# Moving one input load ahead in a DMA queue, and regrouping the reads of an output bank, in a Mamba2 + maxout kernel

## The chip, the cores and the metric

The kernel runs on one core of a Trainium2 chip. The metric is device time of one execution in microseconds (us); the median of three runs of the kernel before is 284.18 us (284.13 to 284.55). Engines are called as in the profile: PE (TensorE matmul), PEld (its weight loads), DVE (VectorE), ACT (ScalarE), POOL (GpSimd), SP (SyncE, which here only issues DMAs). An "SPq" row is the issue of a DMA by SP's sequencer, not its transfer.

## The reference

Two stages follow each other. The first is a chunked state-space scan over 4 sequences, 8 heads, 768 tokens, head width 32 and state width 16. The second is a feed-forward layer with a maximum over three products, on 3072 tokens of width 256:

```
cum = cumsum(log(clip(a)));  L = exp(cum_i - cum_j), causal
y   = ((C B^T) * L) x  +  (C state) * exp(cum)
state = exp(cum_last) * state + sum_j B_j x_j exp(cum_last - cum_j)
x = y as (3072, 256)
h = max(max(x w1, x w2), x w3)          # d_ff = 768
out = h w_out
```

## The kernel before

**Tiling.** The tokens of every sequence are cut into six chunks of 128 (c = 0 to 5). While the feed-forward of chunk c runs on PE, the scan of chunk c + 1 is threaded between its products. The order of all work is written out by hand: the instructions of each engine stand in the order in which the program calls the functions, and every engine goes through its own list in order. Waits between engines are put in by the framework from the tiles that an instruction reads and writes; a PSUM tile counts as a whole, so a write to one quarter of a bank waits for a read of another quarter.

**Chunk 0's feed-forward** is the loop over n (lines 977 to 1038). Among its products it issues the loads of chunk 2 through SP at n = 3 (lines 1011 to 1017) and n = 11 (line 1026): `B`, two weight pieces (`fetch`), the first half of the decay rows `L` (`decay_load`, 1 MB), the eight small loads of `E` (`last_load`), the second half of `L`, `x`, and `C`. `C` has a single buffer (`raw_C`, line 125), so its load of chunk 2 waits until PE has transposed chunk 1's `C` (`scan_tc`, line 428, at n = 11).

**Chunks 1 to 5** follow plans of words (lines 1054 to 1077): FIRST for chunk 1, STEADY for 2 to 4, LAST for 5. One row of a plan is one step k = 0 to 5. The first row of FIRST and the rows k = 3 to 5 of STEADY are

```
"E w tc g L load c e m01"                  # FIRST, k = 0
"E 1 w x2 D L D 1 m23"                     # FIRST, k = 1
"E 2 z1 D D L A D D"                       # STEADY, k = 3
"E 1 y 4 z1 D D L n23 z1"                  # STEADY, k = 4
"E z2 D L 1"                               # STEADY, k = 5
```

- `E` is `early` (line 668): eight products into the banks sumA (one buffer) and sumB (two), then the ACT copy of line 678 and the DVE additions of lines 679 to 681.
- `L` is `late` (line 684): six more products into the same banks, then on even k the ACT copy of line 690, on odd k the DVE maximum of line 707 (`raised`), which read sumA; and the DVE addition of line 695. Another maximum over the other three quarters (line 707 again, 128x768) is put off to the next pop.
- a digit pops that many put-off DVE instructions; `w` is `weight_sums` (DVE line 634, then POOL lines 640 to 643).
- `tc` transposes `C` of the next chunk (line 424), `g` transposes a piece of a weight (723, ACT copy 727), `c` scales that transpose into `CT` (ACT, 439), `e` takes exp of `E` (ACT, 443), `load` issues the loads two chunks ahead.
- `m` and `n` words are the causal masks on POOL (`decay_masks`, line 398); `x` and `z` words are the exponentials of the decays (`decay_part`, ACT, line 405, four instructions a part), which follow the masks of the same tile.
- `y` are the scan's output products (lines 520 and 533).
- `D` is `down_next`: for chunks 1 to 4 it calls `down_seven` (line 793), one seventh of the output product for a pair of sequences u. The sevenths come in the order p = 1, 7, 5, 6, 2, 4, 3, in one PSUM bank `o` of four quarters (line 791 has the quarter of each; p = 2 adds to the quarter of p = 1, p = 4 and 3 to those of 7 and 5). Two pairs make fourteen `D` words per chunk. In STEADY the seventh `D` (p = 3) stands in k = 2, the eighth and ninth (p = 1 and 7) side by side in k = 3, the twelfth and thirteenth (p = 2 and 4) side by side in k = 4, and the fourteenth (p = 3) in k = 5.

In `down_seven` the bank `o` is read at four of the sevenths: after p = 1 by the ACT copy of line 807, after p = 6 by three DVE additions (line 812) of which each takes the result of the one before, after p = 2 by the ACT copy of line 814, and after p = 3 by the DVE addition of line 816, which is followed by the DMA to the output.

Of the kernel before, what the change touches and what calls it, by code (L numbers as in the profile page):

```python
# [19 lines left out]
def kernel(  # L20
# [70 lines left out]
    def ffn_bank(shape, name):  # L91
        turn["ffn"] += 1
        if shared["ffn"] and turn["ffn"] % 3:
            return bank("sumB", 2, shape, name)
        return bank("ffn", 1, shape, name)
# [26 lines left out]
    def load(c, name):  # L122
        src, w = sources[name]
        t = blocks[c][name] = raw.tile(
            [P, BH, w], FP32, tag="raw_" + name, bufs=1 if name == "C" else 2,
            name="raw_" + name)
        nc.sync.dma_start(
            out=t, in_=src[:, :, c * P:(c + 1) * P, :].rearrange("b h s n -> s (b h) n"))
# [70 lines left out]
    def decode():  # L199

        first, second = decode_steps()
        first()
        unsigned.append(second)

    def sign():

        unsigned.pop(0)()
# [69 lines left out]
    def from_last(rows, cum, name):  # L277

        fj = passing(cum)
        for w in range(cum.shape[1]):  # L280
            nc.scalar.activation(
                fj[0:rows, w], cum[0:rows, w], AF.Exp, bias=cum[0:rows, w, P - 1:P], scale=-1.0)
        return fj
# [23 lines left out]
    def decays(c):  # L307
        Ls[c] = att.tile([P, NB, NH, P], FP32, tag="L", name="L")
        return Ls[c]
# [73 lines left out]
    def decay_load(c, pairs=(0, 2)):  # L383
        L = decays(c) if 0 in pairs else Ls[c]
        for b in pairs:
            nc.sync.dma_start(
                out=L[:, b:b + 2].rearrange("j b h i -> j (b h) i"),
                in_=cums[b * NH:(b + 2) * NH, c, :].partition_broadcast(P))

    def last_load(c):  # L390
        E = blocks[c]["E"] = raw.tile([HN, NB, P], FP32, tag="E", name="E")
        rows = cums[:, c].rearrange("(b h) s -> h b s", h=NH)
        for h in range(NH):
            nc.sync.dma_start(out=E[h * N:(h + 1) * N], in_=rows[h].partition_broadcast(N))
# [143 lines left out]
    def first_own(bs):  # L538

        y = att_bank([P, KD, 2, P], "y")  # L540
        for b in bs:
            for h in range(NH):
                t, q = divmod(h, QH)
                nc.tensor.matmul(
                    out=y[q * D:(q + 1) * D, t, b % 2], lhsT=blocks[0]["x"][:, b * NH + h],
                    rhs=L0[:, b, h], start=(b % 2 == 0 and t == 0), stop=True,
                    tile_position=(0, q * D), skip_group_check=True)
        if 0 not in yT:
            yT[0] = ffn.tile([P, KD, BLK], FP32, tag="yT", bufs=3, name="yT")
        r = bs[0] // 2  # L550
        nc.scalar.copy(
            out=yT[0][:, :, r * HB:(r + 1) * HB], in_=y.rearrange("p t b i -> p t (b i)"))
# [29 lines left out]
    def h_of(c):  # L582
        if c not in hT:
            hT[c] = ffn.tile([P, NF, BLK], FP32, tag="h", name="h")
        return hT[c]

    def group(bank, i, f, halves):

        for r in halves:
            for k in range(KD):  # L590
                nc.tensor.matmul(  # L591
                    out=bank[:, r * HB:(r + 1) * HB],
                    lhsT=w_sb[i][:, k, f * P:(f + 1) * P],
                    rhs=yT[0][:, k, r * HB:(r + 1) * HB],
                    start=(k == 0), stop=(k == KD - 1), skip_group_check=True)

    def whole_group(bank, i, f):
        for k in range(KD):
            nc.tensor.matmul(  # L599
                out=bank, lhsT=w_sb[i][:, k, f * P:(f + 1) * P], rhs=yT[0][:, k],  # L600
                start=(k == 0), stop=(k == KD - 1))
# [59 lines left out]
    def pop(n):  # L661
        while n and later:
            later.pop(0)()
            n -= 1
# [97 lines left out]
    def right(p, pair):  # L762

        def part(k, d):
            w = based["G"] if pair == 0 else wo_sb[:, 2 * pair - 2:2 * pair]
            return w[:, k, d * P:(d + 1) * P]

        if p in (1, 2, 4):
            return part(*{1: (0, 0), 2: (1, 0), 4: (1, 1)}[p])
        return seven[p][:, pair]  # L770
# [22 lines left out]
    def down_seven(c, u, p):  # L793

        if p == 1:
            held["o"] = ffn_bank([P, 4, P], "o")
            held["du"] = ffn.tile([P, 3, P], FP32, tag="du", bufs=1, name="du")
            held["out"] = ffn.tile([P, 2, DM], FP32, tag="ob", bufs=2, name="ob")
        o, du, ob = held["o"], held["du"], held["out"]
        flat = ob.rearrange("p b m -> p (b m)")  # L800
        for pair in range(NQ + 1):
            x = sides[c][p] if pair == 0 else zs[c, pair - 1][p]
            nc.tensor.matmul(  # L803
                out=o[:, SLOT[p]], lhsT=x[:, u * P:(u + 1) * P], rhs=right(p, pair),
                start=(p == 1 and pair == 0), stop=True, skip_group_check=True)
        if p == 1:
            nc.scalar.copy(out=du[:, 0], in_=o[:, 0])
        if p == 6:
            for to, one, two in (
                    (du[:, 1], o[:, 1], du[:, 0]), (du[:, 2], o[:, 2], du[:, 1]),  # L810
                    (flat[:, 3 * P:4 * P], o[:, 3], du[:, 2])):
                nc.vector.tensor_tensor(out=to, in0=one, in1=two, op=ALU.add)
        if p == 2:
            nc.scalar.copy(out=flat[:, 0:P], in_=o[:, 0])
        if p == 3:
            nc.vector.tensor_tensor(
                out=flat[:, P:3 * P].rearrange("p (s m) -> p s m", s=2), in0=o[:, 2:4],
                in1=du[:, 1:2].to_broadcast([P, 2, P]), op=ALU.add)
            nc.sync.dma_start(
                out=out.rearrange("(b s) m -> s b m", s=S)[c * P:(c + 1) * P, u::2],  # L820
                in_=ob)
# [126 lines left out]
    def part(c, n=1):  # L948
        for _ in range(n):
            if parts.get(c):  # L950
                decay_part(*parts[c].pop(0))

    def first_tokens():
        from_js = by_token(R, fj, "from_js", 1.0, att_bank)
        for c in range(1, NC):
            ncum[c], from_j[c] = ncums[:, :, c], from_js[:, :, c]
# [20 lines left out]
    for n in range(NF * 3):  # L977
        j, g = divmod(n, 2)
        q, i = divmod(j, 3)
        f = 2 * q + g  # L980
        if n == 0:
            pair = [ffn_bank([P, BLK], "up") for _ in range(2)]
            group(pair[0], 0, 0, (0,))
            first_own((2, 3))
            group(pair[1], 0, 1, (0,))
            for p, ff in zip(pair, range(2)):
                group(p, 0, ff, (1,))
        if j > 0:
            p = ffn_bank([P, BLK], "up")
            whole_group(p, i, f)  # L990
        else:
            p = pair[g]
        if i == 0 and g == 0:
            m = ffn.tile([P, 4, HB], FP32, tag="m", name="m")
        if n in (13, 14, 16, 17):
            pop(2)
        mg = m[:, 2 * g:2 * g + 2].rearrange("p r t -> p (r t)")
        if i == 0:
            nc.scalar.copy(out=mg, in_=p)
        else:  # L1000
            nc.vector.tensor_tensor(
                out=mg if i == 1 else h_of(0)[:, f], in0=mg, in1=p, op=ALU.max)
        if g == 0 and n <= 16:
            sign()
            if n <= 14:
                decode()
        if n == 1:
            fj = from_last(R, a_sb, "fj")
        if n == 3:
            first_tokens()  # L1010
            load(2, "B")
            fetch()
            fetch()
            decay_load(2, (0,))
            last_load(2)
            decay_load(2, (2,))
            load(2, "x")
            decay_masks(1, (0, 1))
        if n == 9:
            decay_masks(1, (2, 3))  # L1020
        if n in (5, 7, 9, 11, 13, 14, 15, 16):
            part(1)
        if n == 11:
            transposed(1)
            scan_c(1)
            load(2, "C")
        if n == 12:
            scan_e(1)
            scan_cd(1)
            scores(1, 0)  # L1030
        if n == 15:
            shared["att"] = False
            scores(1, 2)
            places()
            weight_sums(0)
        if n == 17:
            decode()
            weight_sums(1)
# [136 lines left out]
```

## Time and profile before

| | |
|---|---|
| median of three runs | 284.18 us |
| profiled execution | 283.26 us, of which the span is 281.2 us |
| PE busy | 259.7 us (92%) |
| DVE, ACT, POOL busy | 167.9, 115.7, 108.6 us |
| chain that ended last | PE 87%, DMA 3%, DVE 3%, ACT 3% |
| mean granted TensorE clock | 0.981 |

The span runs from the first instruction to the last of the profiled execution; the 2.1 us between it and the execution's own time lie around it. PE is the engine to watch: the other engines idle a third of the span or more, so their time counts only where PE waits for them. Times in the rows below are microseconds from the start of the span; the second number of a timeline row is what the row took, from its first start to its last end where it merges several instructions.

### The profile page before, as it was taken

To read this page: it belongs to the slowest core of one execution; us is meant where nothing else is said; L and a number is where in the kernel's file an instruction comes from. 1 tells how busy PE (TensorE), PEld (TensorE's weight loads), DVE (VectorE), ACT (ScalarE), POOL (GpSimd) and SP (SyncE) were. 2 spreads that over 40 slices of the span, in tenths; PEclk is the share of its full clock that TensorE was granted. 3 is DMA by queue.
4 is the path that set the end of the run, shared out by engine and by line. 5 is a ranking of instruction groups with operands and counts; after the bars stand their busy time and mean duration, and the time that the engine had idled before them with its cause. 6 is when DMAs were issued, how large, how long until landed. Compare 5 with 4: busy or idle time off the path is not lost.

```text
span 281.2 us, 5499 instructions
## 1 busy us (share of the span) xinstructions
PE 259.7 (92%) x2122; PEld 210.1 (75%) x2122; DVE 167.9 (60%) x330; ACT 115.7 (41%) x312; POOL 108.6 (39%) x140
## 2 busy tenths in 40 slices
PE   6889999990799999999989999989999999999995
PEld 4665344470688788988878988878988888989984
DVE  2585878985088925277565687447586556633430
ACT  2777588840356434822236822047530121100102
POOL 5163665458249892726043543082240124000000
PEclk9999999996599999999999999999999999999999
DMA  7989979979969200859301979001001001010012
GB/s 86 198 278 289 271 144 165 258 189 172 222 135 132 50 2 0 213 168 134 53 2 28 281 110 143 2 3 38 3 0 37 2 0 40 0 37 2 0 37 75
DMA packets 105049, 28.13 MB, mean 100 GB/s; under 512 B 75328, under 2 KB 101952, under 8 KB 105024
## 3 DMA queue, kind: packets, MB, share of 16 engines
q1 hardware_dynamic: 104144, 27.14, 47.9%
q10 hardware_dynamic: 880, 0.66, 0.7%
q8 instruction: 16, 0.26, 0.4%
q14 instruction: 9, 0.07, 0.1%
HBM read 24.54 MB, written 3.24 MB: 99 GB/s over the span
## 4 chain that ended last, share of the span: by engine, by line
PE 87%; DMA 3%; DVE 3%; ACT 3%; issue 1%; POOL 1%; POOLq 0%; DVEq 0%
PE sumB L655 18%; PE o L803 17%; PE sumA L655 14%; PE up L599 8%; PE s L497 5%; PE o L869 5%; PE o L848 4%; DMA raw_C<-in_C_dram 3%; PE y L533 3%; PE fold L736 2%; PE y L520 2%; PE up L591 1%; PE spread L334 1%; PE trC L424 1%; PE trB L424 1%; PE A L465 1%
## 5 line engine op out<-in xcount | busy, mean ns | idle before, releaser
L405 ACT ACTIVATE L<-L,ncums 128x128 f32<-128x128 f32 x160 | 50.0, 393 | 2.7 <-POOL L L398 2.7
L678 ACT COPY eu<-sumA 128x256 f32<-128x256 f32 x30 | 11.2, 372 | 85.1 <-PE sumA L655 82.2
L655 PE MATMUL sumA<-yT,w 128*128 128x256 f32 x120 | 37.1, 391 | 0.0
L655 PE MATMUL sumB<-yT,rb 128*128 128x256 f32 x108 | 33.3, 390 | 0.0
L759 POOL TENSOR_TENSOR rb<-h 128x256 f32<-128x256 f32 x16 | 11.6, 728 | 52.3 <-DVE h L707 44.8
L505 DVE TENSOR_TENSOR L<-s,L 128x512 f32<-128x512 f32 x46 | 29.3, 681 | 1.9 <-PE s L497 1.9
L599 PE MATMUL up<-yT,w 128*128 128x512 f32 x64 | 29.1, 600 | 0.2
L187 POOL TENSOR_TENSOR w_u<-w_u,w_r 128x512 uint32<-128x512 uint32 x12 | 15.9, 1322 | 28.1 <-DVE w_u L181 18.3
L679 DVE TENSOR_TENSOR eu<-sumA,eu 128x256 f32<-128x256 f32 x30 | 12.6, 421 | 22.9 <-ACT eu L678 22.9
L695 DVE TENSOR_TENSOR m<-sumB,eu 128x512 f32<-128x512 f32 x15 | 10.4, 691 | 24.2 <-PE sumB L655 24.1
L655 PEld LDWEIGHTS sumB<-yT,rb 128*128 128x128 f32 x108 | 20.0, 192 | 4.9 <-DVE m L681 1.6
L655 PEld LDWEIGHTS sumA<-yT,w 128*128 128x128 f32 x120 | 20.1, 193 | 3.8 <-issue 1.3
L599 PEld LDWEIGHTS up<-yT,w 128*128 128x128 f32 x64 | 11.6, 190 | 14.7 <-issue 11.7
L398 POOL TENSOR_SCALAR_AFFINE_SELECT L<-L 128x1024 f32<-128x1024 f32 x20 | 22.3, 1137 | 0.0
L655 PE MATMUL sumB<-ys,w 128*128 128x256 f32 x60 | 18.0, 382 | 0.0
L655 PE MATMUL sumA<-ys,rb 128*128 128x256 f32 x60 | 17.8, 379 | 0.0
L655 PE MATMUL sumB<-ys,rb 128*128 128x256 f32 x60 | 17.8, 379 | 0.0
L497 PE MATMUL s<-CT,BT 32*128 32x256 f32 x192 | 14.8, 399 | 1.4 <-ACT CT L439 1.4
L707 DVE SCALAR_TENSOR_TENSOR h<-m,rb 128x768 f32<-128x768 f32 x15 | 14.8, 984 | 0.3
L680 DVE TENSOR_TENSOR v<-sumB,eu 128x256 f32<-128x256 f32 x30 | 12.7, 425 | 3.5 <-PE trB L424 0.5
L484 POOL TENSOR_TENSOR S<-S,old 128x256 f32<-128x256 f32 x4 | 4.1, 1018 | 26.0 <-DVE S L476 25.9
L695 DVE TENSOR_TENSOR rb<-sumB,eu 128x512 f32<-128x512 f32 x15 | 10.4, 692 | 6.2 <-PE sumB L655 6.2
(149 smaller groups left out, 526.9 us busy)
## 6 DMA issues: line engine op xcount, KB each, us to landing
L<-cums SPq DMA_DIRECT2D x10, 1024.0 KB, 8.4
rb<-in_moe_w_dram SPq DMA_DIRECT2D x9, 512.0 KB, 6.6
raw_x<-in_x_dram SPq DMA_DIRECT2D x6, 512.0 KB, 7.4
out_dram<-ob SPq DMA_DIRECT2D x10, 256.0 KB, 2.5
raw_B<-in_B_dram SPq DMA_DIRECT2D x6, 256.0 KB, 4.8
raw_C<-in_C_dram SPq DMA_DIRECT2D x6, 256.0 KB, 6.2
rb<-in_moe_w_out_dram SPq DMA_DIRECT2D x3, 512.0 KB, 4.9
E<-cums SPq DMA_DIRECT2D x40, 32.0 KB, 4.1
```

Source lines behind the costliest of these rows:

```text
L187: nc.gpsimd.tensor_tensor(out=u, in0=u, in1=r, op=ALU.add)
L398: nc.gpsimd.affine_select(out=Ls[c][:, b], in_=Ls[c][:, b], pattern=[[0, NH], [1, P]], compare_op=ALU.is_ge, fill=MASKED, base=0, channel_ ...
L405: nc.scalar.activation(L[:, b, h], L[:, b, h], AF.Exp, bias=ncum[c][:, b * NH + h:b * NH + h + 1], scale=1.0)
L497: nc.tensor.matmul(out=s[:, i].rearrange("j g i -> j (g i)"), lhsT=st["BT"][rows, b], rhs=st["CT"][rows, b].rearrange("p g i -> p (g i)"), ...
L505: nc.vector.tensor_tensor(out=M, in0=s, in1=M, op=ALU.mult)
L599: nc.tensor.matmul(out=bank, lhsT=w_sb[i][:, k, f * P:(f + 1) * P], rhs=yT[0][:, k], start=(k == 0), stop=(k == KD - 1))
L655: nc.tensor.matmul(out=bank[:, half], lhsT=left(p, k), rhs=sides[c][p], start=(first and half == 0), stop=True, skip_group_check=True)
L680: nc.vector.tensor_tensor(out=v, in0=B[:, 1], in1=eu[:, 1], op=ALU.add)
L695: nc.vector.tensor_tensor(out=t[:, 0:2], in0=B, in1=eu[:, 1:2].to_broadcast([P, 2, HB]), op=ALU.add)
L707: nc.vector.scalar_tensor_tensor(out=out, in0=one, scalar=0.0, in1=two, op0=ALU.max, op1=ALU.max)
L803: nc.tensor.matmul(out=o[:, SLOT[p]], lhsT=x[:, u * P:(u + 1) * P], rhs=right(p, pair), start=(p == 1 and pair == 0), stop=True, skip_grou ...
L869: nc.tensor.matmul(out=o, lhsT=left_[:, b * P:(b + 1) * P], rhs=right_, start=(z == 0), stop=(z == 7), skip_group_check=True)
```

## The change

Two edits. In the loop over n, the loads of `E`, of the second half of `L` and of `x` for chunk 2 move from n = 3 to n = 11, behind that of `C`; on SP's queue `C` so stands right behind the first half of `L`. In `down_seven`, the ACT copy that read the bank after p = 1 is made after p = 6, ahead of the three additions, and the one that read it after p = 2 is made after p = 3, ahead of the last addition. What is computed stays the same: no product between p = 1 and p = 6 writes the first quarter, nor one between p = 2 and p = 3.

```
-        if p == 1:
+        if p == 6:
             nc.scalar.copy(out=du[:, 0], in_=o[:, 0])
-        if p == 6:
             for to, one, two in (
                     (du[:, 1], o[:, 1], du[:, 0]), (du[:, 2], o[:, 2], du[:, 1]),
                     (flat[:, 3 * P:4 * P], o[:, 3], du[:, 2])):
                 nc.vector.tensor_tensor(out=to, in0=one, in1=two, op=ALU.add)
-        if p == 2:
+        if p == 3:
             nc.scalar.copy(out=flat[:, 0:P], in_=o[:, 0])
-        if p == 3:
             nc.vector.tensor_tensor(
                 out=flat[:, P:3 * P].rearrange("p (s m) -> p s m", s=2), in0=o[:, 2:4],
                 in1=du[:, 1:2].to_broadcast([P, 2, P]), op=ALU.add)
...
             decay_load(2, (0,))
-            last_load(2)
-            decay_load(2, (2,))
-            load(2, "x")
             decay_masks(1, (0, 1))
...
             transposed(1)
             scan_c(1)
             load(2, "C")
+            last_load(2)
+            decay_load(2, (2,))
+            load(2, "x")
```

More of the change, by code (lines that the diff above doesn't have):

```diff
@@ L805, in down_seven @@
                 start=(p == 1 and pair == 0), stop=True, skip_group_check=True)
-        if p == 1:
+        if p == 6:
             nc.scalar.copy(out=du[:, 0], in_=o[:, 0])
-        if p == 6:
             for to, one, two in (
@@ L812, in down_seven @@
                 nc.vector.tensor_tensor(out=to, in0=one, in1=two, op=ALU.add)
-        if p == 2:
+        if p == 3:
             nc.scalar.copy(out=flat[:, 0:P], in_=o[:, 0])
-        if p == 3:
             nc.vector.tensor_tensor(
@@ L1014 @@
             decay_load(2, (0,))
-            last_load(2)
-            decay_load(2, (2,))
-            load(2, "x")
             decay_masks(1, (0, 1))
@@ L1026 @@
             load(2, "C")
+            last_load(2)
+            decay_load(2, (2,))
+            load(2, "x")
         if n == 12:
```

## The prediction

> **What bounds the kernel now.** I read the engine shares of the page first, then what PE waited for (total, times, longest).
>
> ```profile
> PE 259.7 (92%) x2122; PEld 210.1 (75%) x2122; DVE 167.9 (60%) x330; ACT 115.7 (41%) x312; POOL 108.6 (39%) x140
> ```
>
> ```profile
> PE trC L424 <- DMA raw_C<-in_C_dram: 9.2, 1, 9.2
> ...
> PE o L803 <- ACT ob L814: 2.3, 3, 1.0
> PE o L803 <- ACT du L807: 1.4, 4, 0.4
> ```
>
> PE is busy for 92% of the span, so only its idle time can be won. The three waits are those that the change touches: 9.2 us once for chunk two's C, and 2.3 + 1.4 = 3.7 us in seven waits for the two ACT copies. The chain of waits goes through the first:
>
> ```profile
> 62.58 9.63 DMA raw_C<-in_C_dram
> ...
> 72.34 1.08 PE trC L424 x4
> ```
>
> The end of the kernel hangs on the load of C from its issue at 62.58 to its landing at 72.21. Then the same place cut into stretches (length, then busy time of PE, PEld, DVE, ACT and POOL with counts, granted clock, DMA share, GB/s):
>
> ```profile
> 66.00:72.00 6.00, 0.00 (x0) 0.00 (x0) 1.05 (x3) 0.00 (x0) 5.30 (x7) 0.50 1.30 127
> 72.00:76.00 4.00, 3.66 (x13) 3.33 (x14) 0.00 (x0) 1.42 (x3) 0.05 (x1) 0.50 0.85 240
> ```
>
> They show a second cost: the clock falls to 0.50 during the wait and is still there up to 76. From 72.2 to 76.0 PE does in 3.8 us what takes 1.9 us at full clock. Wait and slow clock together are 9.2 + 1.9 = **11.1 us**. POOL, though, worked through the wait (5.30 of 6 us), and what it did there did not need C: it will not come sooner.
>
> **The load.** SP's queue, and then times from issue to landing (the last number), of the first half of L, the last E and chunk three's B and C:
>
> ```profile
> 51.14 0.37 SPq L386 DMA_DIRECT2D L<-cums  x1
> 51.56 3.77 SPq L394 DMA_DIRECT2D E<-cums  x1
> ...
> 59.26 0.41 SPq L394 DMA_DIRECT2D E<-cums  x1
> ...
> 62.58 5.49 SPq L127 DMA_DIRECT2D raw_C<-in_C_dram  x1
> ...
> 82.65 0.43 SPq L127 DMA_DIRECT2D raw_B<-in_B_dram  x1
> 83.17 2.22 SPq L127 DMA_DIRECT2D raw_C<-in_C_dram  x1
> ```
>
> ```profile
> L<-cums SPq DMA_DIRECT2D x1, 1024.0 KB, 8.1
> ...
> E<-cums SPq DMA_DIRECT2D x1, 32.0 KB, 2.2
> ...
> raw_B<-in_B_dram SPq DMA_DIRECT2D x1, 256.0 KB, 4.2
> ...
> raw_C<-in_C_dram SPq DMA_DIRECT2D x1, 256.0 KB, 6.1
> ```
>
> C takes the place of the first E, at 51.56. The first half of L, issued at 51.14, lands at 59.2. What C adds behind another load is read from chunk three: B lands at 82.65 + 4.2 = 86.9, C at 83.17 + 6.1 = 89.3, so 2.4 us. C then lands at 59.2 + 2.4 = 61.6. The other bound is the slow C of before, 9.6 us from its issue, with the 3.8 us for which that place in the queue was held: 51.6 + 3.8 + 9.6 = 65.0. PE comes to the transpose 9.2 us before 72.34, at 63.15. I take 61.6, since B and C of chunk three are the same pair of a load behind a load: the wait goes.
>
> Moved behind C are eight E, the second half of L, and x. The last E was issued at 59.26 and landed at 61.5; with C's issue of 2.2 to 5.5 us ahead of it, it lands at 63.7 to 67.0. The half of L and x slip by as much; the masks that want that half run at 86.96 in the rows below, 76 after the gain, and the products with x later still. The loads of chunk three stay behind the same bytes as before.
>
> **What is late next.** The timeline of the same stage:
>
> ```profile
> 42.00 0.60 PE L424 MATMUL trC<-ident,raw_C 128*128 128x128 f32 x4
> ...
> 52.49 1.27 POOL L187 TENSOR_TENSOR w_u<-w_u,w_r 128x512 uint32<-128x512 uint32 x1 [3.85 <-DVE w_u L181]
> 52.86 1.45 DVE L634 TENSOR_TENSOR w<-w,w 128x512 f32<-128x512 f32 x1
> ...
> 66.40 0.69 DVE L634 TENSOR_TENSOR w<-w,w 128x512 f32<-128x512 f32 x1
> ...
> 69.92 2.13 POOL L398 TENSOR_SCALAR_AFFINE_SELECT L<-L 128x1024 f32<-128x1024 f32 x2
> ...
> 76.56 0.69 DVE L695 TENSOR_TENSOR m<-sumB,eu 128x512 f32<-128x512 f32 x1 [9.48 <-PE sumB L655]
> 76.59 0.64 ACT L443 ACTIVATE E<-E 128x512 f32<-128x512 f32 x1
> ...
> 77.69 2.44 ACT L405 ACTIVATE L<-L,ncums 128x128 f32<-128x128 f32 x8
> ...
> 78.82 0.42 DVE L681 TENSOR_TENSOR rb<-sumB,v 128x256 f32<-128x256 f32 x1
> ...
> 79.81 0.59 PE L655 MATMUL sumB<-yT,rb 128*128 128x256 f32 x2
> ...
> 80.96 0.41 DVE L707 SCALAR_TENSOR_TENSOR h<-m,sumA 128x256 f32<-128x256 f32 x1
> ...
> 81.97 0.59 PE L655 MATMUL sumA<-yT,w 128*128 128x256 f32 x2
> ...
> 83.08 0.37 ACT L678 COPY eu<-sumA 128x256 f32<-128x256 f32 x1 [2.94 <-issue]
> ...
> 84.47 0.42 DVE L681 TENSOR_TENSOR m<-sumB,v 128x256 f32<-128x256 f32 x1
> ...
> 85.41 0.59 PE L655 MATMUL sumB<-yT,rb 128*128 128x256 f32 x2
> ...
> 86.96 2.13 POOL L398 TENSOR_SCALAR_AFFINE_SELECT L<-L 128x1024 f32<-128x1024 f32 x2
> ```
>
> The single buffer of C is free when SP comes to it: chunk one's transposes end at 42.6. After 63.15 every row of PE behind the slow clock comes 11.1 us earlier, and these stand against it:
>
> - DVE is through with its older work only at 66.40 + 0.69 = 67.1. From there to the end of L681 it has L695 and three additions, 0.69 + 3 x 0.42 = 1.95 us: 69.1. PE wants that bank of sumB at 79.81 - 11.1 = 68.7. **Wait 0.4.**
> - sumA comes free with L707, which ended 2.1 us after that L681 (81.37 against 79.24): 71.2. PE wants it at 81.97 - 11.1 + 0.4 = 71.3: no wait, or up to 0.9 if POOL, at its weight sums and masks beside which DVE now works, holds DVE up twice by 0.5.
> - ACT stands at the exponentials L405, which need the masks of 69.92 to 72.05: the second four start at 72.05 and end, at 2.44 / 8 each, at 73.3. Only then comes the next L678. The L681 behind it ended 84.89 - 83.08 = 1.8 us after L678's start: 75.1. PE wants its bank 85.41 - 81.97 = 3.4 us after 71.3, at 74.7. **Wait 0.4**, or 0.75 if the masks are held up as well.
>
> Together that is 0.8 to 2.05. Such a hold-up stands in the trace: L634 took 1.45 us at 52.86, beside a POOL addition that ended at 53.76, and 0.69 at 66.40. I take 1.5. [...]
>
> ACT wants E at 76.59 - 11.1 = 65.5 at the earliest. At 63.7 it is in time; at 67.0 it adds up to 1.5. I take nothing, as C's issue in chunk three, the pair used above, took 2.2. The load part is 11.1 - 1.5 = **9.6**, between 7.5 and 10.3.
>
> **The reads of the bank.** All seven waits, 3.7 us, go: no product stands right behind a read of its bank any more. In turn each copy now stands ahead of DVE's additions of the same seventh.
>
> After p = 6, the products of the next `E` at least lie ahead of p = 2: four rows like that of 81.97, some 1.7 us. A copy takes 0.3 and an addition at most the 0.41 that L816 takes for twice the width: 0.3 + 3 x 0.41 = 1.5, hidden; chunk five, where nothing else lies between, may lose 0.1. After p = 3 the fourteenth `D` is different:
>
> ```profile
> 151.02 2.44 ACT L405 ACTIVATE L<-L,ncums 128x128 f32<-128x128 f32 x8
> ...
> 152.49 0.41 DVE L816 TENSOR_TENSOR ob<-o,du 128x256 f32<-128x256 f32 x1
> ...
> 152.89 0.42 DVE L707 SCALAR_TENSOR_TENSOR h<-m,sumA 128x256 f32<-128x256 f32 x1
> ...
> 153.60 0.59 PE L655 MATMUL sumA<-yT,w 128*128 128x256 f32 x2
> ```
>
> ```profile
> L814 ACT COPY ob<-o x8: 253/265/266, 128.1 to 261.5; 128x128 f32<-128x128 f32 x8
> ```
>
> In step k = 5 of chunk two the copy is queued behind eight exponentials that end at 153.46, while the addition ran at 152.49. In the built order the addition waits for the copy: copy (0.265, the middle of min/median/max above) to 153.7, addition (0.41) to 154.1, then on the same engine L707 (0.42) to 154.55, which frees sumA for the next chunk's first product. PE wanted that at 153.60: **0.95 lost**. Chunk three's step has the same words and so the same loss; chunks four and five have no exponentials left there. So the part brings 3.7 - 1.9 - 0.1 = **1.7**, between 1.2 and 3.7 (the last if the two reads did not wait for each other).
>
> [...] No row of before has two such reads side by side.
>
> **The sum.** 9.6 + 1.7 = 11.3 us off the profiled execution's 283.26: 272.0. That execution lies 0.9 below the median of 284.18; against the median I forecast **272.9**.
>
> **The rivals.**
>
> 1. Everything is covered and no new wait comes: 11.1 + 3.7 = 14.8 off, 269.4. For it: DVE and ACT are 60% and 41% busy. Against: the rows of 66.40, 69.92 and 151.02. Chance 0.10.
> 2. E lands late behind C, and ACT stands at its exp ahead of the copy L678 for which PE waits. Each us past 65.5 costs up to one: a landing at 67.5 to 69 gives 274.9 to 276.4. For it: the queue's place at 51.56 was held for 3.8 us. Against: C's 2.2 in chunk three. Chance 0.18.
> 3. C itself lands late, at 67: PE waits 3.9 us, and the clock falls again as in the rows of 66 to 76. 11.1 - 3.9 - 1.9 = 5.3 is won, with 0 to 1.7 from the reads: 277 to 279. Chance 0.06.
> 4. C is not ahead in time, as SP is held by something that the rows do not show: the reads alone, 282.5. Against: the buffer is free at 42.6. Chance 0.03.
> 5. Slower: the mechanism of 2 at E's exp on ACT, with a price above the 11.1 + 1.7 = 12.8 us won elsewhere. It decides from a landing of E at 65.5 + 12.8 = 78.3; at 81 the time is 287. C would have to hold the queue for some 17 us, where its longest issue took 5.5. Chance 0.03.
>
> The forecast has 0.58; 0.02 is for what I have not seen. The range **270.0 to 276.0** takes in the forecast's bounds and most of rival 2. Faster by over 0.2% (about what a measurement of this kernel can tell from no change): 0.95; within it: 0.02; slower: 0.03.
>
> **What would show it.** Right: PE no longer waits for raw_C; C is issued near 51.6; the granted clock is 1.00 from 62 to 77; PE waits under a microsecond for DVE's L681 or L707 (now some lines up) between 68 and 76; no wait of o for a copy; and at the end of step k = 5 of chunks two and three PE waits about 1 us for sumA. Wrong: ACT or PE waiting for E's load, a clock of 0.50 after the start, or those two steps without the new wait.

## The result, and the profile after

The kernel after takes 270.47 us in the median of four executions (270.22 to 275.2), beside 284.15 (284.01 to 284.55) for the kernel before on the same chip. The ratio is 0.9513, with a 95% interval of 0.9495 to 0.9532. The ratios here and below, and the times listed for the runs below, leave out executions over 1.5% above the fastest of the same kernel, like the one of 275.2, which at a mean clock of 0.981 lost some 5 us.

The forecast was 272.9 with a range of 270.0 to 276.0. The profiled execution of after took 270.32 us, with a span of 268.6: 12.6 less than the span of before, 12.9 less in its own time. The forecast sum was 11.3.

The page of after, by the engine shares (busy us, share of the span, instructions) and the granted clock in 40 slices:

```profile
PE 257.0 (96%) x2122; PEld 207.4 (77%) x2122; DVE 168.0 (63%) x330; ACT 115.6 (43%) x312; POOL 109.9 (41%) x140
...
PEclk9999999999999999999999999999999999999999
```

PE is busy for 96% of the span instead of 92%, and its clock is full in all 40 slices. What PE waits for in after (total, times, longest):

```profile
PE sumA L655 <- DVE h L707: 1.4, 2, 0.7
...
PE w2T_tp L723 <- issue: 1.0, 1, 1.0
PE sumA L655 <- DVE eu L679: 0.7, 1, 0.7
...
PE sumB L655 <- POOL w L759: 0.4, 1, 0.4
```

The 9.2 us for raw_C and the seven waits of `o` for the two copies are gone from this list. New are the first row and the last two; the row of w2T_tp was 0.50 in before. First the queue of SP in after, then the landing of C (KB, us from issue to landing), then the stage in which before stood still:

```profile
50.31 0.37 SPq L386 DMA_DIRECT2D L<-cums  x1
50.77 3.84 SPq L127 DMA_DIRECT2D raw_C<-in_C_dram  x1
54.66 8.23 SPq L394 DMA_DIRECT2D E<-cums  x8
```

```profile
raw_C<-in_C_dram SPq DMA_DIRECT2D x1, 256.0 KB, 10.3
```

```profile
62.50:66.00 3.50, 3.50 (x22) 2.99 (x21) 2.64 (x5) 3.07 (x8) 2.73 (x4) 1.00 0.56 159
66.00:72.00 6.00, 6.00 (x28) 4.83 (x27) 5.83 (x12) 1.36 (x4) 5.12 (x6) 1.00 1.18 189
72.00:76.00 4.00, 3.26 (x26) 2.04 (x24) 2.91 (x5) 3.85 (x14) 3.92 (x7) 1.00 0.69 206
```

C is issued at 50.77 and lands at 61.1, ahead of its transposes at 63.48. Between 66 and 72, where PE stood for the whole stretch before, it is busy for the whole stretch, at clock 1.00 instead of 0.50. Idle rows of PE come only after 72. The timeline of after shows to whom:

```profile
66.45 0.65 ACT L443 ACTIVATE E<-E 128x512 f32<-128x512 f32 x1
...
70.57 2.59 POOL L398 TENSOR_SCALAR_AFFINE_SELECT L<-L 128x1024 f32<-128x1024 f32 x2
...
72.15 2.45 ACT L405 ACTIVATE L<-L,ncums 128x128 f32<-128x128 f32 x8 [4.79 <-POOL L L398]
...
74.51 0.35 ACT L678 COPY eu<-sumA 128x256 f32<-128x256 f32 x1
...
75.36 0.70 PE L655 MATMUL sumA<-yT,w 128*128 128x256 f32 x2 [0.74 <-DVE eu L679]
...
76.45 0.67 PE L655 MATMUL sumB<-yT,rb 128*128 128x256 f32 x2 [0.38 <-POOL w L759]
```

ACT waits 4.79 us for POOL's masks, runs its eight exponentials, and only then makes the copy L678; PE waits for the DVE addition that stands behind this copy. Where the tail of a row names POOL w L759 as the releaser, DVE's L681 of the same bank sits beside it (75.87 to 76.29), as the prediction had it.

**Where the time came from.** Since PE's list of instructions is the same in both kernels, the shift of one and the same row tells how much has been won by then. One group of products into `o` serves for this: its row has the durations in ns (min/median/max) and then the first and the last start. First the row of before, then that of after:

```profile
L803 PE MATMUL o<-rb,h x96: 275/275/275, 121.2 to 266.8; 128*128 128x128 f32 x96
```

```profile
L803 PE MATMUL o<-rb,h x96: 275/275/275, 112.3 to 254.2; 128*128 128x128 f32 x96
```

The first product of this group starts 8.9 us earlier, and the last 12.6. The stretch up to the first is the load part: **8.9**. The stretch from the first to the last, 145.6 us in before and 141.9 in after, holds all seven copy waits and both new ones: the part of the reads is **3.7**. This stretch is the measure for the experiments on the reads: it does not see what happened near the start.

### The profile page after: what moved, and what is told of

Same layout as the page of the kernel before. It is cut to its first block, busy times and chain, and to the rows that moved or that the text cites. A ratio compares the mean times of both kernels' runs of the same rounds, so it can differ in the third digit from the quotient of the medians.

```text
span 268.6 us, 5492 instructions
## 1 busy us (share of the span) xinstructions
PE 257.0 (96%) x2122; PEld 207.4 (77%) x2122; DVE 168.0 (63%) x330; ACT 115.6 (43%) x312; POOL 109.9 (41%) x140
## 4 chain that ended last, share of the span: by engine, by line
PE 86%; POOL 4%; DVE 3%; ACT 3%; issue 2%; DMA 1%; ACTq 0%; DVEq 0%; POOLq 0%
PE o L803 18%; PE sumB L655 17%; PE sumA L655 14%; PE up L599 9%; PE o L867 5%; PE s L497 5%; PE y L533 4%; PE o L846 3%; PE fold L736 2%; PE y L520 2%; ACT L L405 2%; PE up L591 1%; PE spread L334 1%; PE trB L424 1%; PE A L465 1%
## 5 line engine op out<-in xcount | busy, mean ns | idle before, releaser
L759 POOL TENSOR_TENSOR rb<-h 128x256 f32<-128x256 f32 x16 | 11.6, 727 | 49.4 <-DVE h L707 42.6
L505 DVE TENSOR_TENSOR L<-s,L 128x512 f32<-128x512 f32 x46 | 29.2, 680 | 1.2 <-PE s L497 1.2
L678 ACT COPY eu<-sumA 128x256 f32<-128x256 f32 x30 | 11.2, 372 | 35.2 <-PE sumA L655 35.2
L679 DVE TENSOR_TENSOR eu<-sumA,eu 128x256 f32<-128x256 f32 x30 | 12.6, 421 | 21.8 <-ACT eu L678 21.5
L655 PEld LDWEIGHTS sumA<-yT,w 128*128 128x128 f32 x120 | 19.5, 190 | 7.0 <-DVE h L707 3.6
L655 PEld LDWEIGHTS sumB<-yT,rb 128*128 128x128 f32 x108 | 19.4, 189 | 5.9 <-DVE m L681 1.5
L807 ACT COPY du<-o 128x128 f32<-128x128 f32 x8 | 2.1, 266 | 34.9 <-PE o L803 34.9
L707 DVE SCALAR_TENSOR_TENSOR h<-m,rb 128x768 f32<-128x768 f32 x15 | 15.4, 1026 | 0.3
```

Of the source, the lines that this page charges most:

```text
L505: nc.vector.tensor_tensor(out=M, in0=s, in1=M, op=ALU.mult)
L655: nc.tensor.matmul(out=bank[:, half], lhsT=left(p, k), rhs=sides[c][p], start=(first and half == 0), stop=True, skip_group_check=True)
L679: nc.vector.tensor_tensor(out=eu[:, 1], in0=A[:, 1], in1=eu[:, 0], op=ALU.add)
L707: nc.vector.scalar_tensor_tensor(out=out, in0=one, scalar=0.0, in1=two, op0=ALU.max, op1=ALU.max)
```

## The experiments

The theory after the result was: the load part is as forecast, less small waits in k = 2 behind the masks; the reads part is larger because a wait costs PE more than its idle row shows; the two new waits of sumA come from the ACT copy that stands ahead of the DVE addition. The rivals are named run by run.

### Each part alone

Run 1 is before with the loads moved, and the reads left as they were:

```
             decay_load(2, (0,))
-            last_load(2)
-            decay_load(2, (2,))
-            load(2, "x")
             decay_masks(1, (0, 1))
...
             load(2, "C")
+            last_load(2)
+            decay_load(2, (2,))
+            load(2, "x")
```

> The kernel before with the first edit alone: C of chunk two ahead of E, the second half of L and x; the bank is read as before. Theory (the two edits add up, and the load brings what the shift of PE's rows shows, 8.9 us up to the middle of step k = 2 of chunk one): span about 272.3, time about 275.2; PE never waits for raw_C, clock 1.00 throughout, the seven waits of o for the two copies (0.35 and 0.99 us) still there, and no wait of sumA at the end of steps k = 5. Rival (the load is worth the 11.1 us of wait and slow clock, and the waits in step k = 2 come from the second edit): time about 273, and no wait of PE between 68 and 78.

The ratio is 0.9711 (0.9663 to 0.9759), 276.0 by the 284.17 of before on that chip. It rests on two of the six executions, 274.91 at clock 0.998 and 277.11 at 0.994. The theory's 275.2 lies inside the interval, 274.6 to 277.3, and the rival's 273 outside. PE does not wait for C any more and all seven copy waits are there, with the same 1.4 and 2.3 us as before. The small waits in k = 2 are there too, without the second edit: 0.34 idle ahead of sumA at 75.53, 0.9 by PE's rows. The group of rows used above:

```profile
L803 PE MATMUL o<-rb,h x96: 275/275/275, 115.0 to 260.7; 128*128 128x128 f32 x96
```

Its length is 145.7, as in before: the load gains nothing in this stretch. The profiled execution is the one of 277.11; in it PE was 1.0 us behind after by 19 us, sat idle for 2.06 us at w2T_tp, and the clock was at half from 63.9 to 67.3. That is why the first row here comes at 115.0, not near 112.

Run 2 is before with the copies moved, and the loads left as they were:

```
-        if p == 1:
+        if p == 6:
             nc.scalar.copy(out=du[:, 0], in_=o[:, 0])
...
-        if p == 2:
+        if p == 3:
             nc.scalar.copy(out=flat[:, 0:P], in_=o[:, 0])
```

> The kernel before with the second edit alone; C is loaded last as before. Theory (a wait of PE costs its idle row plus some 0.27 us of restart: 0.62 for each of five short ones and 1.26 for each of two long ones, so 5.6 gone; two new ones of 0.95 each): 3.7 off, time about 280.5, with the wait of 9 us for raw_C and the clock of 0.50 behind it unchanged. Rival (a wait costs its idle row and no more: 3.7 gone, two new ones of 0.70): 2.3 off, time about 281.9.

It took 280.61, ratio 0.9869 (0.9842 to 0.9895): 3.7 us off, from 3.0 to 4.5. Neither the rival's 281.9 nor the 282.5 that the prediction gave for the reads alone lies in the 279.7 to 281.2 that this makes. The length of the group says the same, 265.0 - 123.0 = 142.0:

```profile
L803 PE MATMUL o<-rb,h x96: 275/275/275, 123.0 to 265.0; 128*128 128x128 f32 x96
```

So the reads bring 3.7 with the load edit and without it. The load alone brings 8.2 by run 1's ratio, from 6.8 to 9.6, which takes in the 8.9: within this scatter the two parts add up.

### The two new waits

Run 3 is after with the DVE addition issued ahead of the ACT copy:

```
         if p == 3:
-            nc.scalar.copy(out=flat[:, 0:P], in_=o[:, 0])
             nc.vector.tensor_tensor(
                 out=flat[:, P:3 * P].rearrange("p (s m) -> p s m", s=2), in0=o[:, 2:4],
                 in1=du[:, 1:2].to_broadcast([P, 2, P]), op=ALU.add)
+            nc.scalar.copy(out=flat[:, 0:P], in_=o[:, 0])
```

> The changed kernel, with the addition after p = 3 issued ahead of the copy of the first quarter, so that the copy waits for the addition and not the other way. Theory (the two new waits of sumA are the addition standing in front of L707 behind a copy queued behind eight exponentials): both waits of 0.70 go and each is worth 0.95, so 1.9 us off the changed kernel, time about 268.6. Rival (the copy, now late itself, holds ACT's next copy L678 or the next p = 1 instead): 270.5, with waits of PE on ACT in their place.

It took 267.87, 268.33 and 268.39, ratio 0.9436 (0.9406 to 0.9466): confirmed. Step k = 5 of chunk two in after, and the same place in this kernel:

```profile
140.27 2.44 ACT L405 ACTIVATE L<-L,ncums 128x128 f32<-128x128 f32 x8
...
142.62 0.25 ACT L813 COPY ob<-o 128x128 f32<-128x128 f32 x1
142.90 0.42 DVE L814 TENSOR_TENSOR ob<-o,du 128x256 f32<-128x256 f32 x1 [1.08 <-ACT ob L813]
143.24 0.41 DVE L707 SCALAR_TENSOR_TENSOR h<-m,sumA 128x256 f32<-128x256 f32 x1
...
143.71 0.70 PE L655 MATMUL sumA<-yT,w 128*128 128x256 f32 x2 [0.70 <-DVE h L707]
```

```profile
141.19 0.41 DVE L813 TENSOR_TENSOR ob<-o,du 128x256 f32<-128x256 f32 x1
...
141.59 0.42 DVE L707 SCALAR_TENSOR_TENSOR h<-m,sumA 128x256 f32<-128x256 f32 x1
...
142.07 0.25 ACT L816 COPY ob<-o 128x128 f32<-128x128 f32 x1
...
142.29 0.59 PE L655 MATMUL sumA<-yT,w 128*128 128x256 f32 x2
```

In after, copy, addition, L707 and the product follow each other from the end of the exponentials, as the prediction wrote it down. In run 3 the addition and L707 are done before the copy starts, and the product does not wait. The copy still sits behind the exponentials, but only the output's DMA wants it. At each of the two places PE's rows moved up by 0.95. The median of these three is 268.33, 2.1 below after; run 10 below repeats it at 268.05, and no run of the study has a lower ratio.

### What a wait costs

Run 4 is after with the second copy back behind p = 2, so that the three waits for it return and the two of sumA go:

```
+        if p == 2:
             nc.scalar.copy(out=flat[:, 0:P], in_=o[:, 0])
         if p == 3:
```

> The changed kernel with only the copy after p = 1 moved to p = 6; the copy after p = 2 stays there. Theory (restart cost 0.27): against the load alone the four waits for the first copy go, 4 x 0.62 = 2.5 us, the three for the second copy stay (0.99, 0.99, 0.35), and no wait of sumA for DVE comes: time about 272.7, slower than the changed kernel by 1.2 (2 x 1.26 + 0.62 - 2 x 0.95). Rival (a wait costs its row only): 4 x 0.35 = 1.4 against the load alone, 0.9 slower than the changed kernel.

Its waits are the expected ones: three for the second copy, none for the first, none of sumA at k = 5. The ratio is 0.9586 (0.954 to 0.9633), which by 284.17 is 271.1 to 273.7. Three executions at clock 1.00 took 271.11, 271.61 and 272.16; the ratio also takes in one of 274.96 at 0.988. That is too scattered to set the theory apart from its rival by time alone, so two more runs put the price to the test. Run 9 is run 3 with the first copy back behind p = 1; run 10 is run 3 again, on the same chip:

```
-        if p == 6:
+        if p == 1:
             nc.scalar.copy(out=du[:, 0], in_=o[:, 0])
+        if p == 6:
             for to, one, two in (
```

> This is e3_add_first with the first ACT copy back right after p = 1, so that four of the seven waits return, each with an idle row of about 0.35 (1.4 together), and nothing else. Theory (a wait costs more than its row: 0.62 for a row of 0.35, as rows of the same product stand in before and after): 4 x 0.62 = 2.5 above the unchanged e3_add_first of the same chip; with 268.2 for that, 270.7. Rival (a wait costs its idle row, as the prediction had it): 1.4 above, 269.6. Only executions at clock 1.00 are compared for this. In the trace PE's rows behind the fourth wait should stand about 2.5 later by the theory and 1.4 later by the rival, against e3_add_first.

> e3_add_first unchanged, as the other side of f1_short_waits on the same chip: 268.2 (267.9 to 268.4 at clock 1.00), no wait of sumA at the end of the steps k = 5, about 2.5 below f1_short_waits by the theory and 1.4 below by the rival.

Run 9 took 270.85 to 272.56 with a median of 271.49, run 10 took 267.57 to 268.91 with a median of 268.05: 3.4 apart, where the theory had 2.5 and the rival 1.4. Each scatters by over 1 us, so the trace has to decide. The waits of run 9, and the group by which run 9 and then run 10 are compared in the trace:

```profile
PE o L803 <- ACT du L807: 1.6, 4, 0.4
```

```profile
L803 PE MATMUL o<-rb,h x96: 275/275/275, 112.0 to 254.8; 128*128 128x128 f32 x96
L803 PE MATMUL o<-rb,yT x64: 272/275/377, 107.0 to 254.1; 128*128 128x128 f32 x64
...
L803 PE MATMUL o<-rb,ys x48: 272/275/377, 110.9 to 250.6; 128*128 128x128 f32 x48
```

```profile
L803 PE MATMUL o<-rb,h x96: 275/275/275, 112.8 to 252.8; 128*128 128x128 f32 x96
...
L803 PE MATMUL o<-rb,ys x48: 272/275/275, 111.7 to 248.7; 128*128 128x128 f32 x48
```

From the first row of the group to the last it is 142.8 in run 9 and 140.0 in run 10. Four waits with idle rows of 1.6 us together cost 2.8: 0.3 each beyond the row. The rival, that a wait costs its row, falls. PE has no other idle row over 0.1 us in this stretch, in either run. Run 4's length is 143.2 (115.7 to 258.9), 3.2 above run 10, for three waits with 2.3 of idle rows: again 0.3 each beyond. And before minus run 10 is 145.6 - 140.0 = 5.6, for seven waits with 3.7.

The rest shows in the rows themselves. One of the short waits in before, with the pairs ahead of and behind it; then the same instructions in after:

```profile
134.19 0.38 PE L803 MATMUL o<-rb,yT 128*128 128x128 f32 x2
...
135.60 0.49 PE L803 MATMUL o<-rb,ys 128*128 128x128 f32 x2 [0.35 <-ACT du L807]
...
136.59 0.60 PE L655 MATMUL sumA<-yT,w 128*128 128x256 f32 x2
```

```profile
125.31 0.38 PE L803 MATMUL o<-rb,yT 128*128 128x128 f32 x2
...
126.20 0.39 PE L803 MATMUL o<-rb,ys 128*128 128x128 f32 x2
...
127.10 0.60 PE L655 MATMUL sumA<-yT,w 128*128 128x256 f32 x2
```

From the first row to the last it is 2.40 in before and 1.79 in after: 0.61 for an idle row of 0.35. One matmul of this form takes 0.275 and a pair 0.38, so the next one starts 0.11 after the one ahead of it. The idle row begins only when, by the profile, the last matmul has run out, 0.275 - 0.11 = 0.17 after the point where another would have started. And the first matmul behind a wait takes 0.377 (the largest of rb,ys in run 9; 0.275 in run 10, where there are no such waits), 0.10 more. 0.35 + 0.17 + 0.10 = 0.62.

### How late C may land

Run 5 is after with C behind the eight E:

```
             scan_c(1)
-            load(2, "C")
             last_load(2)
+            load(2, "C")
             decay_load(2, (2,))
```

> The changed kernel with C of chunk two issued behind the eight E instead of ahead of them. C is then issued near 59.7 into a queue that has run empty and lands some 4 to 6 us later, at 63.7 to 65.8, where PE comes at 63.5. Theory (the next limit of this stage is ACT, which stands at the exponentials L405 until POOL's masks are done near 73, so that PE has about 1.1 us to give): a wait for raw_C of 0.3 to 2.3 us appears and the two waits of 0.74 and 0.38 us in step k = 2 shrink or go; time within 1 us of the changed kernel, 270 to 271.5, clock 1.00. Rival (PE is bound by itself behind the transpose): every us by which C is late is added, up to 272.8, and the waits in step k = 2 stay.

Run 6 has C behind E and the second half of L, on the same chip:

```
             scan_c(1)
-            load(2, "C")
             last_load(2)
             decay_load(2, (2,))
+            load(2, "C")
             load(2, "x")
```

> The changed kernel with C behind E and behind the second half of L, but still ahead of x. The half of L, issued near 60.4, lands near 67, C 1.6 to 2.4 us behind it: 68.6 to 69.4. Theory (the load part is the wait plus the clock that falls in it): PE waits 5 to 6 us for raw_C, the clock falls to 0.50 some 3 us into the wait and stays there for a few us of work, the waits in step k = 2 are gone: about 5.5 + 2 - 1.1 more than the changed kernel, 276 to 277. Rival (x alone was what held C up in the kernel before, and L counts for little): under 272.

Run 5 took 269.93, 270.11, 270.46 and 270.88, as after does: E ahead of C brings nothing, and C behind E costs nothing that can be seen. That agrees with the theory's time. Whether C made PE wait in these four is not shown. In the profiled execution (275.16) C landed at 65.4, and PE came to its transposes only at 67.61, 4 us late, after half clock from 16.7 to 27.0. The first half of L was issued 1.25 later there than in after, so by an estimate from these rows C lands near 64.1 without that stretch, half a us after PE comes. So small a wait can't tell the theory from its rival. The waits of 0.74 and 0.38 in k = 2 are there unchanged with E issued ahead of C, so E's landing is not their cause.

Run 6 took 274.62 to 276.73, 275.8 by its ratio of 0.9725 (0.9677 to 0.9774): close to the theory's 276 to 277, and the rival's (under 272) falls. Its list of waits, and the same three stretches:

```profile
PE trC L424 <- DMA raw_C<-in_C_dram: 4.3, 1, 4.3
```

```profile
62.50:66.00 3.50, 0.30 (x2) 0.00 (x0) 3.33 (x6) 0.97 (x2) 2.92 (x4) 0.90 1.14 166
66.00:72.00 6.00, 4.87 (x16) 4.27 (x17) 1.18 (x3) 2.62 (x5) 5.37 (x7) 0.50 1.14 179
72.00:76.00 4.00, 4.00 (x20) 3.53 (x19) 2.98 (x7) 2.73 (x10) 0.00 (x0) 0.99 1.07 274
```

It is a smaller picture of before: PE waits 4.3 us, and the clock is at 0.50 from 66 to 72. The small waits of k = 2 are gone, covered by the long one. Against run 5 it is 5.1 slower by the two ratios. By PE's rows against after, the wait costs 4.5 and the slow clock 2.4; the small waits save 1.75 and a shorter idle time at w2T_tp 0.6, which leaves 4.5.

### What is late next

Run 7 is run 3 with the masks of chunk two's first half (word m01) moved ahead in chunk one's plan, right behind the products of word E:

```
-        "E w tc g L load c e m01",
+        "E m01 w tc g L load c e",
```

> The changed kernel with the addition ahead of the copy after p = 3 (as in e3_add_first), and with the masks of chunk two's first half (word m01) moved in chunk one's step k = 0 from its end to right behind the products, so that POOL makes them before the four weight sums. Theory (ACT's exponentials and, behind them, the copy L678 wait for these masks): L405 starts near 69.5 in place of 72.2, the two waits of PE in step k = 2 (0.74 and 0.38, less what the wait of w2T for nothing shown took) go, 0.5 to 1.3 us off e3_add_first: 267.1 to 267.9. Rival (the weight sums, now 2.2 us later on POOL, hold up the products that read them at 72.1): a wait of PE for POOL L643 of 0.3 to 1 us in place, time as e3_add_first or above, 268.3 to 269.

A miss: it took 267.60, 267.76, 267.97 and 268.32, no less than run 3 against before on its own chip (its ratio is 0.9457, 0.9415 to 0.9499; run 3 had 0.9436). The masks' waits, 0.74 and 0.38 in run 10's profile of the same kernel as run 3, are gone, but PE then waits for DVE in the same stage:

```profile
PE sumA L655 <- DVE h L707: 0.5, 1, 0.5
PE sumB L655 <- DVE rb L681: 0.4, 1, 0.4
```

DVE was busy for 97% of 66 to 72 in after already (5.83 of 6 us): behind the masks it is the next limit of this stage, and moving POOL's work alone wins nothing. From the third transpose into w2T_tp (61.10 in after) to the product behind the last small wait (76.95), PE takes 15.8 us in run 7 as in after; run 10 takes 15.6, and run 3, whose own profile has none of the masks' waits, 15.2.

Run 8 is run 7 with chunk zero's x loaded ahead of the first weight piece, against the wait for x near 16 us that some profiles show (2.4 us in run 2, 1.6 in run 5):

```
     load(0, "C")
-    fetch()
     load(0, "x")
     fetch()
     fetch()
+    fetch()
```

> e6_masks_early with x of chunk zero issued ahead of the first weight piece. Some traces show PE waiting 1.3 to 2.4 us for that x near 14, with a clock of 0.50 for 7 to 10 us behind it. Theory (x lands at 14.2 where PE comes at 14.6, so a late landing stops PE, and the slow clock behind it is what lifts some executions by 3 to 5 us): no wait of PE at L465 in any profile, the highest of its times is within 2 us of its lowest, median 267 to 269. Rival (the first weight piece, now some 2.4 us later, is late for its decoding and for the first product at 18.6): a wait there, 269 to 271, with the slow clock as often as before.

Neither time came: it took 272.88 to 273.74, 0.965 (0.9615 to 0.9684), above the rival's 269 to 271 too. The rival's mechanism did come. The wait for x is gone, but another of 1.9 us stands at 15.4 to 17.3 (s for DVE's L of L505); L505 stands on DVE behind the decoding of the first weight piece (L181), for whose load ACT waited 2.36 us. All six executions have a granted clock of 0.981, and the profiled one has half clock from 17.6 to 27.9.

## Why the prediction was right, and where it was off

- **The wait for C, 9.2, and the slow clock behind it, 1.9: right.** PE's rows behind the slow clock are 10.6 earlier, 11.1 but for the 0.5 of the next point; raw_C is in no list of after's waits. C landed at 61.1, forecast 61.6; the other bound, 65.0, is excluded. Run 6 shows the price of the pair when C is late.
- **An unforeseen 0.5.** PE's idle time at w2T_tp grew from 0.50 to 0.97. No step of the prediction had this; the last section says what goes with it.
- **E at 63.7 to 67.0, taken at no cost: right.** C's issue held the queue for 3.84 us, not the 2.2 that the prediction took as likelier, but by an estimate from its issue near 62.4 and 2.3 us to landing, the last E still landed at 64.7. ACT's exp runs at 66.45 without a wait, and run 5, where E goes first, is not faster. Rival 2 did not come about.
- **The small waits, 1.5 of 0.8 to 2.05: right in sum, wrong in place.** By the shift of PE's rows they cost 1.7. At L681 the forecast had 0.4; L681 ended at 69.17 (forecast 69.1), but PE came later by the 0.5 above and lost 0.2. At sumA behind L707 it lost 0.1. The wait behind the masks was forecast as 0.4 to 0.75; it came as 0.8 at sumA and 0.6 at the bank of sumB, since the masks ended at 73.16 and not at 72.05. They started at 70.57 instead of 69.92, as POOL's weight sum L642 ahead of them took 0.91 where its neighbours take 0.45. Then the two took 2.59 us instead of 2.13, and DVE's L707 beside them took 1.84 where the same form takes 0.96 at 144.29. Both took longer side by side; what slows them, no run shows. The measured 1.7 lies between the 1.5 and the upper end of 2.05.
- **Load part 9.6: it brought 8.9**, namely 11.1 - 0.5 - 1.7.
- **The two new waits of sumA, 0.95 each: right**, in place, cause and size. Run 3 takes the cause away, and the rows move by 0.95 at each. That the addition waits for the copy, no row of before showed; after shows it, with 1.08 us of idle time ahead of L814, released by ACT's L813. Whether it waits for the read of the bank or for the write into the same `ob`, no run tells.
- **"All seven waits, 3.7 us, go": this term failed, by its size.** All went, but they were worth 5.6: the idle rows, and 0.27 more for each. The new waits had been priced from the time at which the product could start, which holds all of the loss; the old ones by their idle rows, which do not. Priced alike, the old ones give 3.7 + 7 x 0.27 = 5.6.
- **Reads part 1.7: it brought 3.7**, 5.6 - 1.9. The forecast's upper end of 3.7 had been worked out from another cause (no wait between the two reads), which runs 2 and 3 rule out. Chunk five's 0.1 can't be made out.
- **The sum.** 8.9 + 3.7 = 12.6 of span instead of 11.3. Of the 2.4 us between 272.9 and 270.47, 1.6 is this sum in the execution's own time (12.9 for 11.3), and 0.8 is that before's profiled execution lay 0.9 under its median, but after's only 0.15. That the time still lies inside the range is in part luck: a load part 0.7 too high and a reads part 2.0 too low partly cancel.
- **The rivals.** The time lies nearer to rival 1 (269.4) than to the forecast, but not by rival 1's cause: new waits of 1.7 + 1.9 us did come. Rivals 3, 4 and 5 did not occur.

## What to carry to other kernels

Price a wait on PE from one product's start to a later product's start, in both kernels, not by the idle row, which here fell short by some 0.27 us a wait; and price the waits that go and those that come by the same measure. Two reads of one bank by two engines are best issued so that the one that others wait for comes first: the copy behind eight exponentials, which had cost 0.95 us at each of two places, was harmless in run 3, once it stood behind the addition. When a long wait goes, look for engines that worked through it: here POOL's masks and DVE's additions took back 1.7 of 11.1 us.

## What the runs showed of the hardware

**Idle times of PE of 1.3 to 2.4 us were followed by half clock in five profiles.** Near 17 us the clock is full in some profiles and half in others, though PE's list of instructions is the same. The stretch from 17 to 27 in after, and in run 2 (the clock is the number right behind the busy times of the five engines):

```profile
17.00:27.00 10.00, 9.30 (x90) 6.10 (x82) 6.28 (x13) 6.47 (x14) 4.38 (x4) 1.00 0.84 249
```

```profile
17.00:27.00 10.00, 9.29 (x91) 6.17 (x84) 3.43 (x7) 2.30 (x4) 2.33 (x2) 0.51 0.89 239
```

PE is as busy in both, but the second ran at half clock. In the profiles with such a stretch PE had been idle shortly before it for 1.3 (run 4), 1.6 (run 5), 1.9 (run 8) and 2.4 us (run 2), in each of the four some 3 to 5 us after another 1.35 us (s for ACT's CT), and in run 1 for 2.06 ahead of the stretch at 63.9. Yet the 1.35 alone, which every profile has between 11.9 and 13.7, was not followed by one in after, nor were the 1.5 at w2T_tp in run 3, the 1.2 in run 10 and the 0.97 in after. The stretches lasted 3.4, 6.8 or some 10.2 us (63.9 to 67.3 in run 1, 65.3 to 72.1 in run 6, 65.8 to 76.1 in before, 16.5 to 26.8 in run 2). A stretch of some 10.2 us cost some 5 us: in run 5 the profiled execution, with one, took 275.2, and the four at a mean clock of 0.998 or more took 269.9 to 270.9; the 275.2 of after, at a mean clock of 0.981, lies as far above the 270.3, but has no profile. In run 2 the wait for C took up most of this cost: PE was 5.8 us behind before at 58, but 1.8 at C's transposes, as the wait was 5.8 instead of 9.2. Removing that wait so also laid open a spread that it had hidden (284.0 to 284.6 in before, 270.2 to 275.2 in after). What starts these stretches is only seen together with the idle times, and run 8 did not get rid of them.

**PE's idle time at w2T_tp**, for which the profile names no releaser, was 0.50 in before, 0.97 in after, 1.5 in run 3, 1.2 in run 10, 0.6 in run 7 and 2.1 in run 1. It stands each time ahead of the same transpose, and it goes with a transfer that is none of the kernel's own loads. The profile of after lists it under a queue of the kind "instruction" (packets, MB, share of 16 engines):

```profile
q8 instruction: 17, 0.28, 0.4%
```

Its packets have 16 KB. In the trace one of them ends 1.3 to 1.7 us before PE goes on in each of the eight profiles with the idle time: at 59.65 ahead of 61.10 in after, 59.29 ahead of 60.61 in before, 61.77 ahead of 63.18 in run 1. In the four profiles without it (runs 2, 4, 5 and 8) PE gets there 2.1 to 3.0 us after the packet's end. So PE may be waiting there for this packet, which comes later or earlier among the loads. That is the author's inference from this coincidence in twelve profiles; no run moved the packet, and the cause is not shown.
